# Token weights in two parts, q and k copied at once, and most turns of u and late x moved to DMA transposes, in a new order

## Chip, cores and metric

The kernel runs on one core of a Trainium2 chip. The metric is device time in microseconds of one execution. A profile shows one execution, which has its own time and a span from its first to its last instruction.

## What is computed

Chunked attention, then a mixing layer over tokens and channels. B = 8 batches, H = 8 heads, S = 576 tokens, D = 64; DM = H x D = 512.

```python
q_c, k_c, v_c = (t.reshape(B, H, 9, 64, D) for t in (q, k, v))       # 9 chunks of 64 tokens
attn = softmax(q_c @ k_c.transpose(0, 1, 2, 4, 3) / 8)
x = (attn @ v_c).reshape(B, H, S, D).transpose(0, 2, 1, 3).reshape(B, S, DM)
theta = x @ w_theta
y = einsum('ts,bsd->btd', w_tok_r, x * cos(theta)) + einsum('ts,bsd->btd', w_tok_i, x * sin(theta))
u = x + y
out = u + maximum(u @ w_ch, 0)
```

## The kernel before

The batches go in four pairs (p = 0 to 3). The 1152 tokens of a pair are 9 tiles of 128 rows, j = 0 to 8: tiles 0 to 3 are batch one, 5 to 8 batch two, tile 4 holds the last 64 tokens of each. Attention and theta work on groups of tiles: A is tiles 0 and 1, B 2 and 3, M the shared tile 4 alone, C 5 and 6, D 7 and 8. Everything that TensorE multiplies is fp16, sums are fp32 in PSUM.

The order of the work is written out by hand: `ORDER` is a list of steps `kind.pg.slot` (p the pair, g the group or tile, slot one of three wide PSUM buffers of two banks or of two thin ones of one bank). The program is built in this order, so each engine gets its instructions in it, and so does each DMA queue: POOL's (all loads that cast fp32 to fp16) and SP's (weights r, stores, moves, transposes). `tc.manual_schedule()` adds only the waits between engines. Buffers come from pools with fixed numbers of buffers; a tile waits until the one that held its buffer is done with.

The steps, with the lines of the profile:

- `q`, `k`, `v` (L174, L182): two POOL DMAs each, for one group. `lt`, `lc` (L202): the weights w_theta and w_ch.
- `lw.00` (L191, L192): w_tok_r comes as fp32 by SP's queue into wraw and wend; `cw` (L198, L199): ACT casts it into wnat. `lw.01` (L194, L195): w_tok_i comes as fp16 by POOL's queue.
- `init` makes the identity on POOL, `ones` fills constants on DVE, `new` takes x, zr, zi of a pair, `D` (L157) is two idle matmuls on a blank tile.
- `TW` (L225): 30 turns of token weights on TensorE into PSUM; `twd` (L241, L243) and `twa` (L241) copy them to wT by DVE and ACT.
- `T` (L259): turns q and k of a group on TensorE into one PSUM buffer, 32 small matmuls (16 for M). `tq` and `tk` (L277, L279) copy q by DVE and k by ACT (both by DVE for M) into two tiles.
- `S` (L290): scores, 32 small matmuls. `e` (L303): exponentials on ACT. `V0`, `V1` (L323): attention times v for four heads each, with a column of ones for the sums; `v0`, `v1` (L335, L336): reciprocal and product on DVE give x.
- `X` (L354), `x` (L366): turn of x on TensorE, 16 matmuls, and copy by ACT. `Xd` (L375): the same by one DMA transpose on SP's queue.
- `H` (L388): theta, 8 matmuls of 512 columns. `g` (L404, L408): cosine and sine on ACT. `z` (L417 to L426): zr and zi on DVE. `zm` (L431, L432): two SP DMAs bring half of the M tile to the other partitions.
- `Y` (L457): token product of one tile, 9 matmuls of 512 columns; for pair 0 in parts `Ya`, `Yb`, `Yc`. `y` (L465): u = x + y on DVE.
- `U` (L474), `u` (L491, L489): turn of u on TensorE, four matmuls, and copy by ACT (even tiles) or DVE (odd). `Ud` (L482): by one DMA transpose on SP's queue.
- `W` (L497): channel product, 4 matmuls. `w` (L506): relu and sum on DVE. `st` (L521): two SP stores of 128 KB each.

A Y needs zr and zi of all groups of its batch and of M, and all nine blocks of wT in its columns. Before, 16 of the 36 u and 15 of the 20 x groups are turned on TensorE, all q and k too.

Of the kernel before, what the change touches and what calls it, by code (L numbers as in the profile page):

```python
# [602 lines left out]
```

The softmax here doesn't subtract the row's maximum and nothing guards it: scores larger than these inputs give would overflow.

## Time and profile before

| | us |
|---|---|
| median of 3 runs (lowest, highest) | 212.73 (212.34, 214.2) |
| profiled execution: its time | 213.03 |
| profiled execution: span of its instructions | 210.7 |
| busy: TensorE, its weight loads | 191.4, 96.7 |
| busy: DVE, ACT, POOL | 123.6, 111.3, 104.4 |
| DMA: moved, at a mean of | 31.36 MB, 149 GB/s |

POOL's busy time is nearly all its work on 124 load DMAs. A matmul counts as busy from its issue to its modelled end, and they overlap, so the sum of the time of all matmuls is more than TensorE's pace. In the views, PE is TensorE, PEld its weight load, DVE the vector engine, ACT the scalar engine, POOL GpSimd, SP the engine that only issues DMAs; a "q" after a name is its sequencer. The row "PE" of the slices gives the busy share of TensorE in 40 equal slices of 5.27 us, in tenths; "PEclk" is the clock that it was granted, in tenths of full speed. The chain of waits is followed back from the last instruction, and is shown as start, length and what ran. The tile view gives for each engine and line the shortest, median and longest instruction in ns and the first and last start.

### The profile page before, as it was taken

How to read it: one execution, taken by the hardware profiler on the slowest of the kernel's cores; microseconds unless marked ns; L12 is line 12 of the kernel's file. 1: busy time of each engine (PE TensorE's matmuls, PEld its weight loads, DVE VectorE, ACT ScalarE, POOL GpSimd, SP SyncE). 2: the span in 40 equal slices, each digit the busy share in tenths (PEclk: the TensorE clock that was granted, in tenths of full speed). 3: DMA queues.
4: the chain of work that ended last, by engine and by line, in shares of the span. 5: the costliest groups of instructions: out<-in, count | busy, mean ns of one | idle time of the engine just before them, and what ended most of it. 6: DMA issues, size and time to landing. Idle time of an engine off the chain costs nothing.

```text
span 210.7 us, 6370 instructions
## 1 busy us (share of the span) xinstructions
PE 191.4 (91%) x2774; PEld 96.7 (46%) x2774; DVE 123.6 (59%) x240; ACT 111.3 (53%) x119; POOL 104.4 (50%) x130
## 2 busy tenths in 40 slices
PE   7678698897989999999999999999899988999981
PEld 2334444353545654555555545545544424444430
DVE  0014644663959675776884447849886365846451
ACT  2525469635886668777567668793260631500010
POOL 8997889988999898987997000000000000000000
PEclk9965579999999999999999999999999999999999
DMA  6999999999999999999999972423428687626875
GB/s 191 189 149 171 186 156 159 162 157 156 150 147 210 218 160 178 153 213 158 169 186 201 190 106 53 104 50 65 91 56 173 125 173 151 151 59 130 174 155 130
DMA packets 136858, 31.36 MB, mean 149 GB/s; under 512 B 129536, under 2 KB 131648, under 8 KB 136832
## 3 DMA queue, kind: packets, MB, share of 16 engines
q0 software_dynamic: 114176, 15.88, 119.6%
q1 hardware_dynamic: 22656, 15.10, 31.5%
q8 instruction: 21, 0.34, 0.7%
q14 instruction: 5, 0.04, 0.1%
HBM read 33.06 MB, written 9.44 MB: 202 GB/s over the span
## 4 chain that ended last, share of the span: by engine, by line
PE 65%; DVE 9%; ACT 9%; DMA 7%; POOL 6%; issue 1%; SPq 0%; POOLq 0%; ACTq 0%
PE ps_y L457 27%; PE ps_theta L388 14%; PE ps_uw L497 13%; POOL qk L174 5%; DMA v<-in_v_dram 4%; PE ps_x L323 3%; DMA xT<-x 3%; ACT kT L277 3%; PE ps_qkT L259 3%; PE ps_sT L290 2%; DVE qT L277 2%; PE ps_xT L354 2%; DVE x L336 2%; ACT xT L366 1%; PE ps_uT L474 1%
## 5 line engine op out<-in xcount | busy, mean ns | idle before, releaser
L457 PEld LDWEIGHTS <-wT 128*128 128x128 f16 (+1 forms) x360 | 30.7, 100 | 34.4 <-issue 0.8
L457 PE MATMUL ps_y<-zr,wT 128*128 128x512 f16 (+1 forms) x180 | 44.4, 381 | 0.0
L457 PE MATMUL ps_y<-zi,wT 128*128 128x512 f16 (+1 forms) x180 | 42.0, 379 | 0.0
L465 DVE TENSOR_TENSOR u<-ps_y,x 128x512 f16<-128x512 f32 x36 | 24.7, 690 | 27.9 <-PE ps_y L457 27.8
L497 PE MATMUL ps_uw<-wch,uT 128*128 128x512 f16 x144 | 36.3, 380 | 1.2 <-ACT uT L491 0.7
L388 PE MATMUL ps_theta<-wtheta,xT 128*128 128x512 f16 x144 | 36.0, 393 | 1.4 <-DMA xT<-x 1.0
L174 POOL DMA_DIRECT2D qk<-in_q_dram x40 | 34.2, 875 | 4.9 <-issue 1.4
L174 POOL DMA_DIRECT2D qk<-in_k_dram x40 | 34.1, 870 | 2.7 <-DMA wnat<-in_moe_w_tok_i_dram 0.8
L182 POOL DMA_DIRECT2D v<-in_v_dram x40 | 34.1, 879 | 2.3 <-DMA qk<-in_k_dram 0.6
L506 DVE SCALAR_TENSOR_TENSOR o<-ps_uw,u 128x512 f32<-128x512 f32 x36 | 24.8, 689 | 15.8 <-PE ps_uw L497 15.5
L404 ACT ACTIVATE cos<-ps_theta,pihalf 128x1024 f16<-128x1024 f32 (+1 forms) x20 | 20.6, 1032 | 21.4 <-PE ps_theta L388 14.9
L303 ACT ACTIVATE eT<-ps_sT 128x1024 f16<-128x1024 f32 (+1 forms) x20 | 18.5, 939 | 16.9 <-PE ps_sT L290 16.8
L336 DVE TENSOR_TENSOR x<-ps_x,recip 128x512 f16<-128x512 f32 (+1 forms) x40 | 25.5, 638 | 1.4
L388 PEld LDWEIGHTS <-xT 128*128 128x128 f16 x144 | 13.7, 100 | 17.9 <-issue 2.1
L497 PEld LDWEIGHTS <-uT 128*128 128x128 f16 x144 | 13.0, 98 | 16.6 <-DMA uT<-u 1.3
L366 ACT COPY xT<-ps_xT 128x1024 f16<-128x1024 f16 (+1 forms) x15 | 13.9, 931 | 12.2 <-PE ps_xT L354 12.1
L277 ACT COPY kT<-ps_qkT 128x1024 f16<-128x1024 f16 x16 | 16.1, 1018 | 7.7 <-DVE qT L277 4.4
L408 ACT ACTIVATE sin<-ps_theta 128x1024 f16<-128x1024 f32 (+1 forms) x20 | 18.7, 937 | 0.0
L491 ACT COPY uT<-ps_uT 128x512 f16<-128x512 f16 x9 | 5.3, 592 | 24.3 <-PE ps_uT L474 24.2
L277 DVE COPY qT<-ps_qkT 128x1024 f16<-128x1024 f16 x16 | 11.0, 688 | 9.3 <-ACT kT L277 6.6
L259 PE MATMUL ps_qkT<-id,qk 64*128 64x64 f16 x576 | 12.8, 196 | 2.1 <-DMA qk<-in_k_dram 1.3
L335 DVE RECIPROCAL recip<-ps_x 128x8 f32<-128x8 f32 (+1 forms) x40 | 7.9, 197 | 10.5 <-PE ps_x L323 10.2
(43 smaller groups left out, 153.5 us busy)
## 6 DMA issues: line engine op xcount, KB each, us to landing
out_dram<-o SPq DMA_DIRECT2D x72, 128.0 KB, 2.4
qk<-in_q_dram POOLq DMA_DIRECT2D x32, 128.0 KB, 6.2
qk<-in_k_dram POOLq DMA_DIRECT2D x32, 128.0 KB, 6.5
v<-in_v_dram POOLq DMA_DIRECT2D x32, 128.0 KB, 6.7
wraw<-in_moe_w_tok_r_dram SPq DMA_DIRECT2D x1, 1152.0 KB, 5.8
wnat<-in_moe_w_tok_i_dram POOLq DMA_DIRECT2D x1, 576.0 KB, 7.7
qk<-in_q_dram POOLq DMA_DIRECT2D x8, 64.0 KB, 6.4
qk<-in_k_dram POOLq DMA_DIRECT2D x8, 64.0 KB, 6.1
```

The source lines that it names most:

```text
L174: nc.gpsimd.dma_start(nats[p, g][rows, which, r], (q, k)[which][b, :, t0 : t0 + n, :].rearrange("h s d -> s h d"),)
L182: nc.gpsimd.dma_start(v16[rows, slot + r, :, 0:D], v[b, :, t0 : t0 + n, :].rearrange("h s d -> s h d"),)
L259: nc.tensor.transpose(psv[:, r, w, e, j, :], t[half[r], w, j, 2 * e : 2 * e + 2, :].rearrange("s h d -> s (h d)"), id16[half[r], half[r]],)
L277: copy(out=t.rearrange(flat), in_=ps.rearrange(flat))
L336: nc.vector.tensor_tensor(out=st[p]["x"][:, j0 : j0 + n, f * NE * D : (f + 1) * NE * D].rearrange("p c (h d) -> p c h d", h=NE), in0=psv[: ...
L388: nc.tensor.matmul(ps[:, j * DM : j * DM + DM], xT[:, j * NDB + db, :], wtheta16[:, db, :], start=(db == 0), stop=(db == NDB - 1),)
L404: nc.scalar.activation(out=cos[:, 0:n].rearrange("p a e -> p (a e)"), in_=pin, func=AF.Sin, bias=pihalf, scale=1.0,)
L408: nc.scalar.activation(out=sin[:, 0:n].rearrange("p a e -> p (a e)"), in_=pin, func=AF.Sin)
L457: nc.tensor.matmul(ps[rows], wT[:, kt, cols], z[:, jz, :], start=(kt == 0), stop=(kt == 2 * KT),)
L465: nc.vector.tensor_tensor(out=u, in0=st[p].pop(("ps_y", j))[:, 0:DM], in1=st[p]["x"][:, j], op=ALU.add)
L497: nc.tensor.matmul(ps, uT[:, db * P : db * P + P], wch16[:, db, :], start=(db == 0), stop=(db == NDB - 1),)
L506: nc.vector.scalar_tensor_tensor(out=o, in0=st[p].pop(("ps_uw", j)), scalar=0.0, in1=u, op0=ALU.max, op1=ALU.add)
```

## The change

- `load_tok` loads both token weights on POOL's queue, as fp16, in two parts: part 0 (`lw.00`, `lw.01`) holds output tokens 0 to 255, part 1 (`lw.02`, `lw.03`) tokens 256 to 575, with a second DMA for the last 64. The SP loads, wraw, wend and the cast on ACT go.
- `tok_w` turns one part in two steps (`TW.00` to `TW.03`: 16, 20, 24 and 30 matmuls); `tok_w_copy` copies them on DVE alone.
- `qk_copy` copies q and k by one instruction into one tile qkT, by DVE (`tq`, 8 groups) or ACT (`tqa`, 8). The q and k of 3A to 3D are transposed by one SP DMA each (`Td`) from the loaded tile.
- x: 8 of 20 groups are turned on TensorE, copied by ACT (`x`, 4) or DVE (`xv`, 4), and 12 are DMA transposes. u: tile 34 is turned on TensorE, the other 35 by DMA transposes.
- `D` is one idle matmul, and there are 60 (before 14 of two).
- Buffers: nat 8 (before 7), u16 7 (6), uT 5 (4), qkT 4 and 2 (before 3 and 2 each of qT and kT).
- The order is new. POOL loads q of A, B, C, M, k of A and B, w_theta and k of M before it makes the identity; the token weights follow after v.0B.

The first and last lines of the old order are shown, and the whole of the new one.

```diff
--- before.py
+++ after.py
@@ ORDER @@
-ones.00 D.00.0 lw.00 cw.00 D.00.1 init.00 D.00.0 D.00.1 q.0M q.0B q.0A D.00.0 k.0M
-D.00.1 D.00.0 D.00.1 k.0B TW.00.0 twa.00 k.0A D.00.0 T.0M.1 tk.0M D.00.1 D.00.0 tq.0M
-S.0M.2 e.0M lt.00 T.0B.1 T.0A.2 tk.0A tq.0B D.00.1 tq.0A tk.0B S.0A.2 v.0M V1.0M.1 v.0A
-e.0A D.00.0 V0.0M.2 twd.00 S.0B.0 new.00 v1.0M V1.0A.1 v0.0M V0.0A.2 v0.0A v.0B q.1M
-v1.0A lw.01 X.0M.2 e.0B V1.0B.0 X.0A.1 v1.0B x.0M H.0M.2 V0.0B.0 x.0A v0.0B q.0C k.1M
-v.0C H.0A.1 g.0M X.0B.0 z.0M zm.0M x.0B g.0A TW.02.2 H.0B.0 T.1M.1 twa.02 twd.02 TW.01.2
...
-y.36 w.35 W.32.0 w.32 st.35 Ud.36 Y.34.1 y.34 Y.33.0 W.37.1 y.33 W.36.0 w.37 Y.38.1
-st.32 Ud.34 w.36 Ud.33 y.38 st.37 W.34.0 w.34 W.33.1 w.33 st.36 st.34 st.33 U.38.0 u.38
-W.38.1 w.38 st.38 D.00.0
+ones.00 new.00 D.00.0 q.0A D.00.1 D.00.0 D.00.1 D.00.0 D.00.1 D.00.0 q.0B D.00.1 D.00.0
+q.0C D.00.1 D.00.0 D.00.1 D.00.0 D.00.1 q.0M D.00.0 k.0A D.00.1 D.00.0 D.00.1 k.0B
+D.00.0 D.00.1 D.00.0 D.00.1 D.00.0 D.00.1 lt.00 D.00.0 k.0M D.00.1 D.00.0 D.00.1 D.00.0
+D.00.1 D.00.0 D.00.1 D.00.0 D.00.1 D.00.0 init.00 T.0A.0 T.0B.1 tq.0A v.0A S.0A.2 D.00.1
+D.00.0 k.0C tqa.0B v.0M D.00.1 v.0B D.00.0 D.00.1 q.1M lw.02 q.0D D.00.0 D.00.1 S.0B.0
+T.0M.1 tq.0M D.00.0 e.0A V0.0A.2 S.0M.1 e.0B e.0M V1.0A.0 T.0C.1 v0.0A lw.03 v1.0A
+V0.0M.2 D.00.1 D.00.0 lw.01 v0.0M lw.00 V1.0M.0 v1.0M X.0A.2 k.0D xv.0A v.0C tqa.0C
+X.0M.0 V0.0B.1 q.1D V1.0B.2 new.10 v0.0B v.0D D.00.1 q.1C k.1M x.0M H.0M.0 H.0A.1 v1.0B
+X.0B.2 g.0M TW.02.0 k.1D x.0B D.00.0 z.0M g.0A twd.02 v.1M q.1A H.0B.2 k.1C D.00.1
+TW.03.0 z.0A D.00.0 lc.00 twd.03 g.0B z.0B Ya.02.1 S.0C.1 TW.01.2 q.2M TW.00.0 v.1D v.1C
+q.1B twd.00 twd.01 k.2M zm.0M Yb.02 k.1A Yc.02 Ya.01.0 Yb.01 y.02 T.0D.0 e.0C V0.0C.1
+v0.0C v.2M V1.0C.2 Yc.01 Ya.00.1 Yb.00 v1.0C tqa.0D k.1B v.1A X.0C.1 S.0D.2 xv.0C Yc.00
+Ud.02 y.01 e.0D V0.0D.0 v0.0D V1.0D.1 v1.0D H.0C.2 q.2A v.1B X.0D.0 T.1M.1 g.0C y.00
+D.00.0 D.00.1 xv.0D Ud.01 D.00.0 H.0D.0 tq.1M S.1M.1 Ya.03.1 D.00.0 z.0C g.0D Yb.03
+Yc.03 e.1M T.1D.2 tqa.1D z.0D v.2A T.1C.0 Y.06.0 tq.1C S.1C.1 V1.1M.0 y.03 y.06 v1.1M
+S.1D.2 Y.08.1 k.2A e.1C V0.1M.0 q.2B y.08 e.1D V1.1D.1 V0.1D.2 Y.07.0 q.2D Ud.00 v0.1D
+v1.1D q.2C v0.1M k.2B W.02.1 V0.1C.2 V1.1C.1 y.07 w.02 X.1M.0 v1.1C k.2D W.01.0 W.00.1
+Ud.06 Xd.1D x.1M H.1M.0 T.2M.1 Ud.07 v0.1C g.1M w.01 tq.2M T.1A.2 tq.1A Y.05.0 Ud.03
+S.2M.1 S.1A.2 q.3M st.02 w.00 Ud.08 k.2C T.1B.0 Y.04.1 e.2M Xd.1C y.05 tq.1B v.2B e.1A
+st.01 st.00 V1.1A.1 q.3C V0.1A.0 v.2D v0.1A S.1B.2 W.06.0 H.1D.0 e.1B v.2C g.1D y.04
+v1.1A X.1A.2 xv.1A V0.1B.1 W.03.1 k.3M H.1A.2 v0.1B w.06 H.1C.1 g.1A w.03 Ud.05 V1.1B.0
+z.1M W.07.0 v1.1B w.07 W.08.1 V0.2M.2 X.1B.0 w.08 g.1C z.1D st.06 z.1C st.03 T.2A.1
+zm.1M x.1B tqa.2A q.3B W.05.0 H.1B.0 w.05 v.3M g.1B Y.15.1 Ud.04 y.15 new.20 v0.2M z.1B
+st.07 Y.18.0 st.05 k.3C y.18 S.2A.1 T.2D.0 q.3D T.2B.2 Ud.15 st.08 Ud.18 W.04.1 tq.2B
+e.2A tqa.2D Y.17.0 V1.2A.1 z.1A S.2B.2 w.04 V1.2M.0 v1.2M Y.14.1 v1.2A T.2C.0 Xd.2M y.17
+e.2B y.14 Ud.14 st.04 V0.2A.2 v0.2A tqa.2C V0.2B.1 Y.11.0 q.3A S.2C.2 v0.2B S.2D.1 y.11
+V1.2B.0 W.18.1 w.18 W.15.0 Xd.2A Y.16.1 v1.2B k.3B T.3M.0 e.2D V0.2D.1 Ud.11 e.2C w.15
+V1.2D.2 Y.10.0 tqa.3M Ud.17 y.16 v1.2D y.10 st.15 st.18 k.3D H.2M.0 W.14.1 Y.13.0 w.14
+Xd.2B Ud.10 g.2M Ud.16 v0.2D Xd.2D Td.3C V1.2C.2 y.13 S.3M.1 k.3A V0.2C.0 v1.2C W.11.1
+Y.12.0 st.14 w.11 H.2A.2 W.17.1 st.11 Ud.13 v0.2C g.2A v.3D H.2B.0 Xd.2C y.12 Ud.12 v.3B
+z.2M W.16.0 w.17 g.2B w.16 st.17 W.13.1 z.2B H.2D.2 H.2C.0 z.2A zm.2M Td.3B new.30 w.13
+Y.22.0 g.2D y.22 Y.21.1 g.2C z.2C e.3M st.16 y.21 st.13 Td.3A W.10.0 V0.3M.2 v.3C w.10
+Td.3D S.3B.0 e.3B z.2D st.10 S.3C.1 e.3C Ud.21 Y.23.1 W.12.0 V1.3M.0 y.23 V0.3B.1 Ud.22
+Ud.23 v0.3M v0.3B v1.3M Y.20.1 w.12 S.3A.2 V0.3C.1 y.20 st.12 V1.3C.0 W.21.0 v0.3C w.21
+Y.25.1 st.21 v1.3C Ud.20 W.22.0 v.3A y.25 W.23.1 w.22 S.3D.1 e.3A V1.3B.2 Xd.3M V0.3A.0
+v0.3A v1.3B st.22 Y.24.0 w.23 Ud.25 st.23 y.24 e.3D V1.3D.1 V0.3D.0 V1.3A.2 v1.3A Y.26.1
+v0.3D y.26 Xd.3B Ud.26 v1.3D Xd.3C W.25.0 H.3M.2 w.25 Y.28.1 Xd.3A y.28 st.25 H.3B.0
+Ud.24 Xd.3D W.20.0 W.26.1 g.3M z.3M w.26 Ud.28 g.3B z.3B H.3A.1 w.20 st.20 Y.27.1 st.26
+g.3A y.27 Ud.27 H.3D.2 z.3A g.3D W.28.0 zm.3M w.28 z.3D W.24.1 H.3C.0 w.24 Y.33.0 st.24
+y.33 W.27.1 w.27 st.28 g.3C Ud.33 Y.30.0 y.30 Ud.30 z.3C st.27 Y.31.1 y.31 Ud.31 Y.32.0
+y.32 Ud.32 W.30.1 w.30 Y.38.0 y.38 W.33.1 st.30 w.33 st.33 W.32.0 Ud.38 w.32 Y.36.1 y.36
+Ud.36 W.31.0 w.31 st.31 st.32 Y.37.1 y.37 Y.35.0 W.36.1 y.35 w.36 Ud.37 Y.34.0 W.38.1
+y.34 Ud.35 W.35.0 w.38 w.35 W.37.1 U.34.0 uv.34 st.36 W.34.0 w.37 D.00.1 D.00.1 D.00.1
+st.38 w.34 D.00.0 st.35 D.00.1 st.37 D.00.0 D.00.1 st.34
@@ -112,7 +112,7 @@
     thin = ctx.enter_context(
         tc.tile_pool(name="thin", bufs=1, space=bass.MemoryType.PSUM)
     )
-    nat = ctx.enter_context(tc.tile_pool(name="nat", bufs=7))
+    nat = ctx.enter_context(tc.tile_pool(name="nat", bufs=8))
     tmp = ctx.enter_context(tc.tile_pool(name="tmp", bufs=3))
     pairp = ctx.enter_context(tc.tile_pool(name="pairp", bufs=1))
     outp = ctx.enter_context(tc.tile_pool(name="outp", bufs=4))
@@ -131,8 +131,6 @@
     wch16 = glob.tile([P, NDB, DM], FP16, name="wch16")
     wT = glob.tile([P, 2 * KT + 1, S], FP16, name="wT")
     wnat = glob.tile([P, KT + 1, 2, S], FP16, name="wnat")
-    wraw = pairp.tile([P, KT, S], FP32, name="wraw")
-    wend = glob.tile([CH, S], FP32, name="wend")
     blank = const.tile([P, DM], FP16, name="blank")
     v16 = glob.tile([P, 2 * NT, H, VP], FP16, name="v16")
 
@@ -153,8 +151,7 @@
 
     def idle(p, i, slot):
         ps = psum1("ps_idle", slot)
-        for r in range(2):
-            nc.tensor.matmul(ps, blank[:, 0:P], blank, start=True, stop=True)
+        nc.tensor.matmul(ps, blank[:, 0:P], blank, start=True, stop=True)
 
@@ -184,66 +181,61 @@
                 v[b, :, t0 : t0 + n, :].rearrange("h s d -> s h d"),
             )
 
-    def load_tok(ri):
+
+
+    def load_tok(i):
+        part, ri = divmod(i, 2)
         ap = (moe_w_tok_r, moe_w_tok_i)[ri]
-        aps = ap[0 : KT * P, :].rearrange("(a p) s -> p a s", p=P), ap[KT * P : S, :]
-        if ri == 0:
...
+        nc.gpsimd.dma_start(
+            wnat[:, 2 * part : 2 * part + 2, ri],
+            ap[part * GT : part * GT + GT, :].rearrange("(a p) s -> p a s", p=P),
+        )
+        if part:
+            nc.gpsimd.dma_start(wnat[0:CH, KT, ri], ap[KT * P : S, :])
 
     def load_w(ap, f16):
         nc.gpsimd.dma_start(f16, ap.rearrange("(a p) e -> p a e", p=P))
 
-    def tok_w(k3, slot):
+
+
+    def tok_w(i, slot):
+        part = i // 2
+        kts = range(KT) if i % 2 == 0 else range(KT, 2 * KT + 1)
+        n = len(kts)
         ps = psum2("ps_wT", slot, FP16)
-        for k in range(3):
-            kt = 3 * k3 + k
...
+        main = ps[:, 0 : n * GT].rearrange("p (k x) -> p k x", k=n)
+        middle = ps[:, 5 * GT : 5 * GT + n * CH].rearrange("p (k x) -> p k x", k=n)
+        for tbs in ((0, 1),) if part == 0 else ((2, 3), (KT,)):
+            for k, kt in enumerate(kts):
+                for tb in tbs:
+                    rows = slice(0, P if tb < KT else CH)
+                    if tb < KT:
+                        to = main[:, k].rearrange("p (c r x) -> p c r x", c=2, r=2)
+                        to = to[:, :, tb % 2]
                     else:
-                        ri, s0 = h, KT * P
-                    nc.tensor.transpose(
...
+                        to = middle[:, k]
+                    for h in range(2):
+                        if kt < 2 * KT:
+                            ri, jl = kt // KT, kt % KT
+                            s0 = (jl // 2) * GT + (jl % 2) * CH + h * P
+                        else:
+                            ri, s0 = h, KT * P
+                        nc.tensor.transpose(
+                            to[half[h]],
+                            wnat[rows, tb, ri, s0 : s0 + CH],
+                            id16[rows, rows],
+                        )
+        st["wT", i] = main, middle
+
+    def tok_w_copy(i):
+        main, middle = st["wT", i]
+        part = i // 2
+        ks = slice(0, KT) if i % 2 == 0 else slice(KT, 2 * KT + 1)
+        nc.vector.tensor_copy(out=wT[:, ks, part * GT : part * GT + GT], in_=main)
+        if part:
+            nc.vector.tensor_copy(out=wT[:, ks, KT * P : S], in_=middle)
 
@@ -265,22 +257,37 @@
                         )
         st[p]["ps_qkT", g] = psv
 
-    def qk_copy(p, g, which):
+    def qk_tile(n):
+        return tmp.tile(
+            [P, 4 * NE * n * CH], FP16, name="qkT", tag=f"qkT{n}",
+            bufs=4 if n == 2 else 2,
+        )
+
+
+
+    def qk_copy(p, g, copy):
         n = 1 if g == "M" else 2
-        ps = st[p]["ps_qkT", g][:, :, which]
-        name = "qk"[which] + "T"
-        t = tmp.tile([P, 2, NE, n, CH], FP16, name=name, tag=f"{name}{n}", bufs=n + 1)
-        st[p][name, g] = t
-        copy = nc.scalar.copy if which and n == 2 else nc.vector.tensor_copy
-        if n == 2:
-            flat = "p r e j c -> p r (e j c)"
-            copy(out=t.rearrange(flat), in_=ps.rearrange(flat))
+        ps, t = st[p]["ps_qkT", g], qk_tile(n)
+        tv = t.rearrange("p (r w e j c) -> p r w e j c", r=2, w=2, e=NE, j=n)
+        if n == 1:
+            flat = "p r w e c -> p (r w e) c"
+            copy(out=tv[:, :, :, :, 0].rearrange(flat), in_=ps[:, :, :, :, 0].rearrange(flat))
         else:
-            copy(out=t[:, :, :, 0], in_=ps[:, :, :, 0])
+            copy(out=t, in_=ps.rearrange("p r w e j c -> p (r w e j c)"))
+        st[p]["qkT", g] = lambda hs, w, e, j, r: tv[hs, r, w, e, j, :]
+
+    def qk_dma(p, g):
+        t = qk_tile(2)
+        nc.sync.dma_start_transpose(
+            t.rearrange("p (a c) -> p a c", c=P),
+            nats.pop((p, g)).rearrange("p w j h d -> p (w j h d)"),
+        )
+        tv = t.rearrange("p (w j e r c) -> p w j e r c", w=2, j=2, e=NE, r=2)
+        st[p]["qkT", g] = lambda hs, w, e, j, r: tv[hs, w, j, e, r, :]
 
     def scores(p, g, slot):
         n = 1 if g == "M" else 2
-        qT, kT = st[p].pop(("qT", g)), st[p].pop(("kT", g))
+        t = st[p].pop(("qkT", g))
         ps = psum2("ps_sT", slot)
         psv = ps.rearrange("p (h j e c) -> p h j e c", h=2, j=2, e=NE)
         for j in range(n):
@@ -289,8 +296,8 @@
                     for r in range(2):
                         nc.tensor.matmul(
                             psv[half[r], h, j, e, :],
-                            kT[half[h], r, e, j, :],
-                            qT[half[h], r, e, j, :],
+                            t(half[h], 1, e, j, r),
+                            t(half[h], 0, e, j, r),
                         )
         st[p]["ps_sT", g] = ps
 
@@ -358,12 +365,12 @@
                     )
         st[p]["ps_xT", g] = psv
 
-    def x_copy(p, g):
+    def x_copy(p, g, copy):
         n = 1 if g == "M" else 2
         psv = st[p].pop(("ps_xT", g))
         xT = tmp.tile([P, 2 * NDB, P], FP16, name="xT")
         st[p]["xT", g] = xT
-        nc.scalar.copy(
+        copy(
             out=xT[:, 0 : n * NDB].rearrange("p a (r c) -> p r a c", r=2), in_=psv
         )
 
@@ -460,7 +467,7 @@
                 )
 
     def add_x(p, j):
-        u = tmp.tile([P, DM], FP16, name="u16", bufs=6)
+        u = tmp.tile([P, DM], FP16, name="u16", bufs=7)
         st[p]["u", j] = u
         nc.vector.tensor_tensor(
             out=u, in0=st[p].pop(("ps_y", j))[:, 0:DM], in1=st[p]["x"][:, j], op=ALU.add
@@ -477,18 +484,15 @@
         st[p]["ps_uT", j] = psv
 
     def u_dma(p, j):
-        uT = tmp.tile([P, DM], FP16, name="uT", bufs=4)
+        uT = tmp.tile([P, DM], FP16, name="uT", bufs=5)
         st[p]["uT", j] = uT
         nc.sync.dma_start_transpose(uT.rearrange("p (a c) -> p a c", a=NDB), st[p]["u", j])
 
-    def u_copy(p, j):
-        uT = tmp.tile([P, DM], FP16, name="uT", bufs=4)
+    def u_copy(p, j, copy):
+        uT = tmp.tile([P, DM], FP16, name="uT", bufs=5)
         st[p]["uT", j] = uT
         psv = st[p].pop(("ps_uT", j))
-        if j % 2:
-            nc.vector.tensor_copy(out=uT, in_=psv)
-        else:
-            nc.scalar.copy(out=uT, in_=psv)
+        copy(out=uT, in_=psv)
 
     def w(p, j, slot):
         uT = st[p].pop(("uT", j))
@@ -529,16 +533,15 @@
         "lt": lambda p, g: load_w(moe_w_theta, wtheta16),
         "lc": lambda p, g: load_w(moe_w_ch, wch16),
         "lw": lambda p, i: load_tok(i),
-        "cw": lambda p, i: cast_tok(),
         "init": lambda p, g: setup(),
         "ones": lambda p, g: fill(),
         "new": lambda p, g: pair(p),
         "TW": lambda p, i, slot: tok_w(i, slot),
-        "twd": lambda p, i: tok_w_copy(i, 0),
-        "twa": lambda p, i: tok_w_copy(i, 1),
+        "twd": lambda p, i: tok_w_copy(i),
         "T": qk_t,
-        "tq": lambda p, g: qk_copy(p, g, 0),
-        "tk": lambda p, g: qk_copy(p, g, 1),
+        "Td": qk_dma,
+        "tq": lambda p, g: qk_copy(p, g, nc.vector.tensor_copy),
+        "tqa": lambda p, g: qk_copy(p, g, nc.scalar.copy),
         "S": scores,
         "e": exps,
         "V0": lambda p, g, slot: attn(p, g, 0, slot),
...
+        "ua": lambda p, j: u_copy(p, j, nc.scalar.copy),
+        "uv": lambda p, j: u_copy(p, j, nc.vector.tensor_copy),
```

## The prediction

> **What bounds the kernel now.** I read the page first: the busy shares, then the slices.
>
> ```profile
> PE 191.4 (91%) x2774; PEld 96.7 (46%) x2774; DVE 123.6 (59%) x240; ACT 111.3 (53%) x119; POOL 104.4 (50%) x130
> ...
> PE   7678698897989999999999999999899988999981
> ...
> PEclk9965579999999999999999999999999999999999
> DMA  6999999999999999999999972423428687626875
> ```
>
> TensorE is the bound from about 62 us on (9s); before that it is not full, its clock is low from slice 3 to 6, and the DMA engines are full until slice 23 (about 120 us), when the last load lands. Two stages, then: a start that waits for loads, and a long stretch in which TensorE's own work sets the pace.
>
> The chain of waits in order of time prices the steps, since back to back steps follow each other there without a gap:
>
> ```profile
> 102.39 0.86 PE ps_uw L497 x4
> 103.26 0.34 PE ps_xT L354 x16
> ...
> 104.94 0.22 PE ps_uT L474 x4
> ...
> 106.49 1.02 ACT kT L277
> ...
> 107.54 0.70 DVE qT L277
> 108.24 0.04 issue
> 108.28 1.89 PE ps_theta L388 x8
> ...
> 130.19 0.57 PE ps_qkT L259 x32
> ...
> 132.34 1.73 PE ps_theta L388 x8
> ...
> 190.53 1.94 PE ps_y L457 x9
> ```
>
> A token product Y (9 matmuls) is 1.94, a theta H (8) 1.73, a channel product W (4) 0.86 to 0.87, a turn of q and k T (32) 0.57, of x X (16) 0.34, of u U (4) 0.22 to 0.23; from other rows of this chain scores S (32) are 0.38 to 0.39, one attention half V (16) 0.25 to 0.26. Groups M cost about half. The three rows at 106.49 to 108.28 show a real stall: kT is copied by ACT, then qT by DVE, one after the other, and theta stands behind.
>
> I lay these prices along the order. From the first token product at 36.71 to the last W at 204.85 the steps add up to 157.6 us; the stretch took 168.1. So 10.5 us are lost there: 3.9 by T.1D at 61.6, 6.0 by 118, 1.2 more at 148 and 2.0 between 165 and 175. The span is 36.7 (start) + 157.6 + 10.5 + 5.9 (last W, add, store, end) = 210.7.
>
> Last, the DMA side: the tile view of uT and the page's issue list.
>
> ```profile
> L482 SPq DMA_TRANSPOSE uT<-u x20: 1188/1213/2321, 114.6 to 199.9; - x20
> ...
> DMA to landing us min/median/max: 2.4/2.4/6.6
> ```
>
> A transpose of u lands 2.4 us after its issue once the loads are over, but the first, issued at 114.6 among them, took 6.6. SP spends 1.2 us on each.
>
> **What the Trainium skill says.** "DMA: Bandwidth & Descriptors", section "Issuing engines are not separate DMA queues": DMAs from SP, ACT and POOL run on the same 16 engines and interleave. The trace agrees: out stores land mostly in 2.2 to 2.5 us after 124, in 5.1 to 7.6 during the loads. The same page, section "SWDGE vs HWDGE vs iDMA": a cast needs GpSimd's queue, a transpose SP's or ACT's; in the trace the fp16 loads are all POOL's, the transposes all SP's. "TensorE: Matmul & The Clock Gate", section "What's actually happening": the array's clock is halved until recent activity releases it. In the windows view the granted clock is 0.50 from 12.35 to 29.42, and the 12 theta matmuls from 25.5 on take 1.82 + 2.69 = 4.5 us in the chain instead of 0.86 + 1.73.
>
> **The change, part by part.**
>
> Turns removed from TensorE. U falls from 16 to 1: 15 x 0.23 = 3.45. X falls from 12 full and 3 M to 6 full and 2 M: 6 x 0.34 + 0.20 = 2.24. T falls from 16 full to 12: 4 x 0.57 = 2.28. Token-weight turns stay 90 transposes. Sum 8.0 us off the 172.2 us of all steps without idle ones. Those after 62 us lie on the full engine and count whole.
>
> Copies. ACT loses the 16 kT (16.1), most x copies (13.9 to about 3.2), 9 uT (5.3), wT (2.4) and the cast of the weights (2.8, and a table load). It gains 7 copies of 2048 columns; by the slope of its rows (597 ns at 512, 1018 at 1024) one is about 1.86, and one M copy of 1.02: 14.0. ACT 111 becomes about 88. DVE loses 19.7 and gains 4 x 1.23 (slope 417 to 688), 3 x 0.69, wT 3.6, x 2.8, u 0.4, so 13.8: 124 becomes 118. Neither bounds. The one-instruction copy takes 1.23 or 1.86 where the pair in turn took 1.72, so T to S is no longer; it only loses the wait between engines (6.6 + 4.4 us in the list of waits, partly under TensorE work). Larger tiles (nat 8, u 7, uT 5, four qkT) cost no time; wraw's room pays.
>
> DMA transposes: 35 u, 12 x and 4 qk of 2048 columns. SP: 35 x 1.2 + 12 x 1.3 + 4 of an unseen length, at least 1.3 and by columns 2.6 to 5, + 80 plain issues x 0.6 = about 115 to 125 of 200 us, so SP isn't full; behind a late one stand stores and transposes. In the built order every SP DMA also waits for the landing of the one eight before it, at 6.6 us latency 8 in 6.6 us, above the need. Between u's add and its W, or x's norm and its H, the new order leaves 6 to 16 us during the loads and 3.5 to 14 after; an Ud needs 6.6 + 1.2 and then 2.4 + 1.2. I find few that are short by 1 to 2 us (W.13, H.2C, H.3B, H.3A, W.35). This I leave in the losses below.
>
> Their share of the loads' engines is not shown by the trace. From below: hidden in the gaps, 0. From above: a u transpose has 512 packets and a full load 1024, spaced 0.88 us, so 0.44 each, or 0.88 if a packet of 256 bytes counts twice. Up to 92 us the order issues 12 u and 2.5 x, so 7.5 us (15 at the dear end). POOL, too, waits for the landing of its load eight before: landings past 7 us slow the loads. Taking the old landings by position for the new list, the loads lie 0 to 3 us ahead of use up to T.2D without any loss, and 5 to 9 with the start and losses that I take. So I count 1 us for 0.44.
>
> Token weights. r no longer comes by SP at 0.7 to 7.3 us beside the first loads, with 2.8 us of ACT work; r and i come by 6 POOL DMAs (before 2), about 0.8 each, behind 25 loads: 4 x 0.8 = 3.2 us more in POOL's queue, with every later load behind them. Token turns move from 8.7 to behind 33 us; half of them (1.8 us) now falls after the first Y.
>
> The start, in POOL's order. The identity is made after 15 loads, near 13.6; T.0A follows near 14.2, S.0A near 16.6, v.0A lands near 22 (as before, 20.9 to 22.4), v.0M near 26, v.0B near 28.5. V0.0B and V1.0B stand ahead of H.0M, so thetas begin near 30 instead of 25.5. ACT then has table 1.3, g.0M 1.3, x.0B 1.0, g.0A 2.1; token turns TW.02 and TW.03 need weights that land near 32 and 35.5. The first Y comes at 38 with a fast clock, 40.3 if thetas run at half clock again (34 idle matmuls keep it up only until about 11). I take 39: 2.3 later than before, with fewer token turns and one more T done.
>
> The sum. From Ya.02 to W.34 the steps add up to 152.1 (157.6 less U 3.45, X 2.24, T 2.50, plus turns 1.8 and four idle matmuls 0.86). Losses: before 10.5, of which some 2 are small change between steps. Fewer ACT to DVE hand-overs and no wait for uT copies should take off 2.5; loads behind transposes add 1: 9. Tail 5.9 as before, since U.34 and its copy stand there like U.38. Span 39 + 152.1 + 9 + 5.9 = 206.0. The profiled execution was 213.03 for a span of 210.7, so + 2.3: 208.3; it lay 0.3 above the median of the runs, so 208.0.
>
> **Rivals.**
> A (forecast, 0.48): as summed, losses 7 to 11: 206 to 210.
> B (0.20): hand-overs go almost entirely, clock warm at the start: 38 + 152.1 + 5.5 + 5.9 = 201.5, time 203.5. For it: ACT falls by 23 us and the chain holds ACT and DVE for 18%. Against: the load slack is thin until 92 us.
> C (0.17): the late thetas run cold, weights land late, first Y at 41.5 and losses 11: 210.5, time 212.5, unchanged. The change then moves work from the stretch to the start.
> D (0.15), slower: the transposes take the loads' place on the DMA engines. Place: from Ud.02 (about 47) to the last load. At 0.88 per u, the loads of T.2D are 15 us late against 9 of slack, 6 lost, and the 6 further u, 4 x and one qk before the loads end add 1 to 2: span 213, time 215. It decides from about 0.7 us per u transpose. For it: the first u transpose took 6.6, and landings rise from 5.8 to 7.7 when 10 SP DMAs come within 9 us (60 to 69). Against: these ten, of 64 to 128 KB as one u is 128, cost 1.9 of later landing and 1.2 of POOL waits, 0.3 each.
>
> **How the numbers follow.** The time is A's, 208.0. A's own range is 206 to 210. To hold 8 in 10 I go from B's centre, 203, to 214.5, short of D's centre: a half of B's and somewhat more than a half of D's chance lie outside. About 1% is what a measurement can tell from no change: below 210.6 is faster, A and B but for a margin: 0.67; above 214.9 slower, D: 0.16; the rest 0.17.
>
> **What would show it.** In the changed profile the first ps_y matmul at 38 to 40; u transposes landing in 5 to 8 us before 120 and 2.4 after; the page's ACT near 88, DVE near 118; PE at 9s from about slice 9 with few waits for ps_x or qkT; the last load landing at 124 to 130. D would show as PE waits for DMA qk or v between 60 and 100 and a last landing past 140; C as a low clock over the thetas and a first Y after 41. I am wrong if the stretch from first Y to last W isn't near 161.

## The result, and the profile after

The changed kernel takes 240.28 us (median of 4, 239.62 to 242.75), the kernel before beside it 212.53 (4 runs): ratio 1.132, 95% interval 1.121 to 1.143. It is 13% slower; 2% faster was forecast. The profiled execution took 239.62, its span is 237.8. Ratios here leave disturbed executions out, so for e12 below ratio and median stand apart, e8 has no ratio, and the profiles of these two are of disturbed executions (e12's of 215.65).

The page: busy shares, then the slices (5.95 us each).

```profile
PE 195.2 (82%) x2514; PEld 92.7 (39%) x2514; DVE 120.1 (50%) x222; ACT 87.4 (37%) x84; POOL 106.9 (45%) x134
...
PE   7847899994999869906999964069979899999994
...
PEclk9988799997699999975899995558999999999999
DMA  7999999999999999999999999999986787555666
```

ACT fell as meant, and TensorE has 260 instructions less. But its 9s have holes up to slice 27 (160 us), at the deepest ones the clock falls to 5, and the DMA engines are at 9 to slice 29 (about 172 us; before, to slice 23, about 121). The last packet of a load comes at 165.6; before, at 121.4.

The shares of the chain of waits by engine, before and after, and rows of the chain after:

```profile
PE 65%; DVE 9%; ACT 9%; DMA 7%; POOL 6%; issue 1%; SPq 0%; POOLq 0%; ACTq 0%
```

```profile
DMA 41%; PE 39%; POOL 12%; issue 2%; DVE 2%; ACT 1%; SPq 1%; ACTq 0%; POOLq 0%
...
79.97 15.88 DMA qk<-in_q_dram
96.15 13.11 DMA qk<-in_k_dram
...
124.49 8.64 DMA uT<-u
...
134.41 9.80 DMA uT<-u
...
144.26 1.90 PE ps_uw L501 x4
...
149.81 6.85 DMA uT<-u
...
156.71 1.89 PE ps_uw L501 x4
158.59 5.45 PE ps_theta L395 x16
```

DMA had 7% of the chain, and has 41%. First loads hold it, 29 us in a row, then u transposes, 6.85 to 9.80 each. Two of the W that follow take 1.9 instead of 0.86, and 16 theta matmuls 5.45 instead of 3.46: the granted clock was 0.50 in the last wait (146.1 to 156.7 us) and 0.60 in the 7 us after it. So this wait of 10.6 us costs 3.0 more in the W and the thetas behind it.

The list of what TensorE waited for (us in total, times, longest), the tile view of uT, and the page's issue list, before and after (last column: median us from issue to landing):

```profile
PE ps_uw L501 <- DMA uT<-u: 13.8, 4, 10.6
PE ps_qkT L251 <- DMA qk<-in_k_dram: 12.7, 6, 6.6
```

```profile
L489 SPq DMA_TRANSPOSE uT<-u x35: 1188/1278/2973, 40.6 to 226.1; - x35
...
DMA to landing us min/median/max: 2.4/6.2/9.8
```

```profile
qk<-in_k_dram POOLq DMA_DIRECT2D x32, 128.0 KB, 6.5
v<-in_v_dram POOLq DMA_DIRECT2D x32, 128.0 KB, 6.7
```

```profile
qk<-in_k_dram POOLq DMA_DIRECT2D x32, 128.0 KB, 8.6
v<-in_v_dram POOLq DMA_DIRECT2D x32, 128.0 KB, 8.9
```

Both sides are late: the loads of k and v take 8.6 and 8.9 (before 6.5 and 6.7). The 18 transposes of u that are issued before the last load packet take 6.2 to 9.8, the 17 after it 2.4 to 4.3; before the change 17 of the 20 came after the loads.

Along the order, with the prices of the prediction, the first Y starts at 36.1 and the last W at 231.4; between them lie 152.1 of steps and 43.2 of losses, which is time beyond the steps' prices. The losses stand at 9.1 at 86 us; 9.2 come at once at T.2B (110 us, loads of 2B), 11.6 at W.13 (157 us, transpose of u.13).

### The profile page after: what moved, and what is told of

The parts are those of the page before. It is cut to its first block, busy times and chain, and to the rows that moved or that the text cites. A ratio compares the mean times of both kernels' runs of the same rounds, so it can differ in the third digit from the quotient of the medians.

```text
span 237.8 us, 5842 instructions
## 1 busy us (share of the span) xinstructions
PE 195.2 (82%) x2514; PEld 92.7 (39%) x2514; DVE 120.1 (50%) x222; ACT 87.4 (37%) x84; POOL 106.9 (45%) x134
## 4 chain that ended last, share of the span: by engine, by line
DMA 41%; PE 39%; POOL 12%; issue 2%; DVE 2%; ACT 1%; SPq 1%; ACTq 0%; POOLq 0%
PE ps_y L464 18%; DMA uT<-u 14%; DMA qk<-in_k_dram 13%; PE ps_uw L501 11%; POOL qk L171 9%; DMA qk<-in_q_dram 7%; PE ps_theta L395 6%; DMA xT<-x 4%; DMA wtheta<-in_moe_w_theta_dram 3%; POOL v L179 1%; PE ps_sT L297 1%; PE ps_qkT L251 1%; POOL wnat L189 1%; ACT eT L310 1%; PE ps_x L330 1%
## 5 line engine op out<-in xcount | busy, mean ns | idle before, releaser
L501 PE MATMUL ps_uw<-wch,uT 128*128 128x512 f16 x144 | 38.4, 400 | 14.4 <-DMA uT<-u 13.8
L464 PE MATMUL ps_y<-zr,wT 128*128 128x512 f16 (+1 forms) x180 | 46.4, 392 | 0.1
L464 PEld LDWEIGHTS <-wT 128*128 128x128 f16 (+1 forms) x360 | 31.7, 102 | 37.6 <-issue 5.3
L464 PE MATMUL ps_y<-zi,wT 128*128 128x512 f16 (+1 forms) x180 | 43.4, 388 | 0.0
L395 PE MATMUL ps_theta<-wtheta,xT 128*128 128x512 f16 x144 | 37.2, 406 | 2.3 <-DMA xT<-x 2.3
L251 PE MATMUL ps_qkT<-id,qk 64*128 64x64 f16 x448 | 11.1, 199 | 16.6 <-DMA qk<-in_k_dram 12.7
L276 ACT COPY qkT<-ps_qkT 128x2048 f16<-128x2048 f16 x7 | 13.1, 1865 | 28.0 <-PE ps_qkT L251 28.0
L276 DVE COPY qkT<-ps_qkT 128x2048 f16<-128x2048 f16 x5 | 6.1, 1222 | 27.5 <-PE ps_qkT L251 27.5
L154 PE MATMUL ps_idle<-blank 128*128 128x512 f16 x60 | 18.4, 443 | 1.3 <-DVE pihalf L142 1.2
L251 PEld LDWEIGHTS <-qk 64*128 64x128 f16 x448 | 8.8, 100 | 20.3 <-DMA qk<-in_k_dram 13.6
L342 DVE RECIPROCAL recip<-ps_x 128x8 f32<-128x8 f32 (+1 forms) x40 | 7.9, 196 | 11.7 <-PE ps_x L330 11.4
```

The lines of the kernel that those rows point to most:

```text
L251: nc.tensor.transpose(psv[:, r, w, e, j, :], t[half[r], w, j, 2 * e : 2 * e + 2, :].rearrange("s h d -> s (h d)"), id16[half[r], half[r]],)
L276: copy(out=t, in_=ps.rearrange("p r w e j c -> p (r w e j c)"))
L395: nc.tensor.matmul(ps[:, j * DM : j * DM + DM], xT[:, j * NDB + db, :], wtheta16[:, db, :], start=(db == 0), stop=(db == NDB - 1),)
L464: nc.tensor.matmul(ps[rows], wT[:, kt, cols], z[:, jz, :], start=(kt == 0), stop=(kt == 2 * KT),)
L501: nc.tensor.matmul(ps, uT[:, db * P : db * P + P], wch16[:, db, :], start=(db == 0), stop=(db == NDB - 1),)
```

## The experiments

Theory 1: loads and transposes together are more than the DMA engines carry in time, so each makes the other late. Theory 2: the transposes are late by themselves, by SP's order and their own length. Theory 3: the new order, weights or copies lose the time.

**Undoing a part of the transposes.** Turns on TensorE and their copies go back into the new order, well ahead of their use.

```diff
 e1: 18 u of pairs 0 and 1      e2: x of 1D, 1C, 2A to 2D, 2M   e3: q, k of 3A to 3D
-Ud.13                          -Xd.2B                          -Td.3C
+U.13.0 uv.13                   +X.2B.0 xv.2B                   +T.3C.2 tq.3C
 e4: e1, e2 and e3 together
```

> The changed kernel, but the 18 u of pairs 0 and 1 are turned on TensorE and copied, instead of by DMA transposes. T1 (each DMA transpose takes about 1 us of the loads' time on the DMA engines, so q, k and v land late and TensorE starves): 18 x 1.1 = 20 us less, last load lands near 145 instead of 165, time 222 to 228. T2 (the transposes only land late themselves, behind the loads and in SP's order, and W waits for them): the W waits of 14 us go, the last load stays past 158, time 224 to 228. T3 (order, weights or copies lose the time): 236 to 242, plus 4 us of turns.

> The changed kernel, but the x of 1D, 1C and pair 2 are turned on TensorE and copied; u and late q, k stay DMA transposes. T1: 6.5 transposes of double size, 13 x 1.1 = 14 us less for the loads, last load near 150, time 226 to 232. T2: only the 2 us of theta waits for x go, last load past 158, time 236 to 239. T3: 240 to 243.

> The changed kernel, but q and k of 3A to 3D are turned on TensorE and copied. T1: two of these four came before the last load, 8 u sizes, so last load near 156, time 233 to 237. T2 (SP held 2.7 to 5.6 us by each of these, 17 us in all, with transposes of u and x behind): W waits after 137 fall by 8 to 10 us, time 228 to 232. T3: no change, 239 to 242.

> The three together: no DMA transpose before pair 2's u; later u and pair 3's x stay DMA transposes. T1 and T2: last load at 120 to 126, few waits for loads or uT, time 205 to 212. T3: 225 or more.

| | time | ratio (interval) | last load packet |
|---|---|---|---|
| after | 240.28 | 1.132 (1.121, 1.143) | 165.6 |
| e1 | 229.89 | 1.081 (1.075, 1.086) | 137.7 |
| e2 | 230.10 | 1.083 (1.075, 1.090) | 156.2 |
| e3 | 238.91 | 1.122 (1.116, 1.129) | 160.9 |
| e4 | 247.51 | 1.154 (1.146, 1.162) | 125.3 |

e1 and e2 gain 10 us each, e3 about 1, which is within its interval: u and x count, q and k hardly. Only two of the four transposes of q and k are issued before the last load packet, at 141.5 and 158.0. In e1 the last load comes 28 us earlier, which theory 2 had excluded, though the time lies above the range of either. e4 frees the loads (125.3), and is the slowest: theories 1 and 2 had said 205 to 212, and it lies where theory 3 had put it, at 225 or more. Its slices and its longest waits:

```profile
PE   8757999999779688996696785953699999999984
...
DMA  8999999999999999999972210600325587745766
```

```profile
ACT uT L497 <- PE ps_uT L483: 33.3, 8, 10.2
...
ACT qkT L278 <- PE ps_qkT L253: 21.2, 5, 13.8
```

The DMA engines have little to do from slice 22 to 30, and TensorE is full of small gaps. They come evenly (4.5 us of losses by 72, 20 by 138, 40 at the end), and ACT and DVE wait long for turns that TensorE has not reached. I read this as an order laid out for transposes that loses by itself when turns are put back by hand; no run with an order of its own for them shows it. So e4 shows that with the new order, the token weights and the copies, but without the transposes, the loads end only 4 us later than before; it says nothing on what early loads are worth.

**Adding transposes to the kernel before.** Idle ones into a spare tile that nobody reads, one (e5) or two (e6) per u; e7 copies the same u in 512 pieces of 256 bytes, without turning.

```diff
+        e = st["extra"][0][:, st["extra"][1] % 8]
+        nc.sync.dma_start_transpose(e.rearrange("p (a c) -> p a c", a=NDB), st[p]["u", j])
 e7:
+        nc.sync.dma_start(e[:, :, 0:P], st[p]["u", j].rearrange("p (a c) -> p a c", a=NDB))
```

> The kernel before, plus 11 DMA transposes of u (128x512, fp16) into a spare tile that nobody reads, each issued when its u is ready, between 45 and 110 us. Nothing waits for them but the reuse of u. T1 (about 1.1 us of the loads' time each): last load at 131 to 134 instead of 120.5; the old order has 9 to 25 us of slack, so time 212.5 to 215. T2 (loads unharmed): last load at 120 to 123, time 212 to 213.5.

> As the dose of 11, with each u transposed twice: 22. T1: last load at 142 to 148, slack used up by k.2A, k.2B and v.2A, time 216 to 226. T2: last load at 120 to 125, time 212 to 215.

> As the dose of 22, but each is a plain SBUF to SBUF copy of the same u in 512 pieces of 256 bytes. If it is the packets, whatever they do: as the 22 transposes. If it is the transpose: last load at 120 to 131, time 212 to 215.

| | time | ratio (interval) | last load packet |
|---|---|---|---|
| e5, 11 | 215.33 | 1.013 (1.011, 1.016) | 142.1 |
| e6, 22 | 227.67 | 1.068 (1.059, 1.076) | 154.2 |
| e7, 22 plain | 217.23 | 1.022 (1.014, 1.029) | 145.1 |

This is theory 1 in the kernel before: transposes that nobody waits for make its loads 21 and 33 us late, and the end with them once the slack is used up.

The price is an estimate. Counted in windows of 2.5 us, the load queue finishes 1167 packets per us where SP is silent, and each 256-byte packet of SP's takes the place of 1.9 of them in the changed kernel, 2.3 in e5, 2.2 in e6, and 1.7 in e7. A u has 512, so a transpose takes 0.83 to 1.0 us of the loads' time. Other ways of counting spread further. A straight line through such windows gives 1.3 to 1.8 packets, about 0.6 to 0.8 us. The end of the loads gives more, and it came later than theory 1 had said, too: before the last load packet lie 14.0 u sizes in e5 and 25.0 in e6, against 1.4 in the kernel before, so the 20.7 and 32.8 us are 1.6 and 1.4 for each added one. About 1 us is all that can be said.

Plain pieces (e7) delay the loads by 24 us where transposes delay them by 33, and cost 2.2% where those cost 6.8%. So the turning isn't needed for the harm, but adds to it. Whether the rest is the small pieces or only the bytes isn't shown: no run copied u in large pieces.

**Fewer packets per load.** q and k read in rows of 2 KB.

```diff
-                (q, k)[which][b, :, t0 : t0 + n, :].rearrange("h s d -> s h d"),
+                (q, k)[which][b].rearrange("h s d -> (h s d)")[t0 * DM : (t0 + n) * DM]
+                .rearrange("(s h d) -> s h d", h=H, d=D),
```

> The changed kernel with one difference: q and k are read in rows of 2 KB that lie together (the first elements of the same batch, in memory order) instead of 64-element rows of eight heads, so a full load of q or k has 128 packets instead of 1024; v is loaded as before. The attention is then of other values than the reference's. Order, turns, copies and all DMA transposes are untouched. Theory 1 (the transposes' small packets take the loads' time on the DMA engines, and the late loads cause the losses): with q and k packets gone the loads end near POOL's own pace, about 110 to 125, the transposes land earlier, and most of the 34 us of unforeseen losses go: 206 to 216, and not slower than the same edit of the kernel before by more than 2%. Theory 2 (SP's order and the transposes' own time are what comes late) and theory 3 (the order, weights and copies lose the time whatever the loads do): 228 or more, and at least 8% above the same edit of the kernel before.

> The kernel before with the same edit: q and k read in rows of 2 KB that lie together, so that the attention is of other values than the reference's. It is the base for the kernel above. Its loads end at POOL's pace, about 105 to 120. All theories: its stretch had only some 4 us of waits for loads, so 207 to 212.

e8 lay between 226.08 and 237.84 (median of 4: 232.99), too spread for a ratio, and its last load came at 150.1 instead of 165.6. Theory 1's numbers failed (206 to 216, loads until 110 to 125); the time lies where theories 2 and 3 had put it. e9: 212.27, 0.998 (0.995, 1.001), last load at 117.5 instead of 121.4.

DMA slices of e9 (5.27 us each), and POOL's row for v from its page (after the last bar: its idle time, and who ended most of it):

```profile
DMA  6999999999999999279999742423428687626875
...
L183 POOL DMA_DIRECT2D v<-in_v_dram x40 | 34.4, 884 | 12.5 <-PE ps_x L324 11.4
```

But for two slices they stand at 9 as before. The windows view shows more: its last two numbers are the mean busy share of the DMA engines, which passes 1 where packets overlap, and GB/s. First before, then e9:

```profile
10.00:50.00 40.00, 33.23 (x645) 18.23 (x643) 20.12 (x46) 22.03 (x25) 34.82 (x43) 0.79 2.42 162
```

```profile
10.00:50.00 40.00, 30.59 (x617) 16.63 (x616) 19.80 (x46) 22.03 (x25) 30.99 (x49) 0.87 1.48 177
```

The share fell from 2.42 to 1.48 while the rate rose from 162 to 177 GB/s, and k lands in 5.1 us instead of 6.5. So the edit did make the loads lighter. That they end little sooner is no sign against it: they run so far ahead that POOL waits 11.4 us in one piece, until 92, for a buffer of v that TensorE still reads, and this is what the two slices show. In e8 TensorE's waits for q and k nearly go (12.7 us for k in the changed kernel), but those for v grow from 3.0 to 8.0, and those for transposes stay (uT 13.7 for 13.8, xT 4.6 for 2.3). Why lighter loads of q and k help the transposes so little is open. The two runs don't support theory 1 in the form that they tested, in which the number of packets is what a load costs.

**Fewer loads.** The same transposes and SP order, 37 of 120 load sizes left out.

```diff
+        if which and (p, g) in SAME:      # pairs 1 and 2, and 3M
+            return
 ...
+        if p >= 2:                        # load_v
+            return
 ...
-                            t[half[r], w, j, 2 * e : 2 * e + 2, :].rearrange(
+                            t[half[r], 0 if same else w, j, 2 * e : 2 * e + 2, :].rearrange(
```

> The changed kernel with 37 of its 120 load sizes left out: k of pairs 1 and 2 and of 3M is not loaded (q is turned twice in its place), v of pairs 2 and 3 is not loaded (that of pairs 0 and 1 stays), so the attention of those is of other values than the reference's. All DMA transposes, their order and all steps of TensorE stay. 37 x 0.88 is 33 us of the loads' time. Theory 1 (loads and transposes together are more than the DMA engines can carry in time): most of the 34 us of losses go, 206 to 218. Theory 2 (SP's order and the transposes' own time): u.13 still stands behind the long transpose of 3C, 226 or more.

> The kernel before with the same loads left out (k of pairs 1, 2 and 3M, v of pairs 2 and 3), so its attention is of other values too. Base for the kernel above. Its waits for loads in the stretch were some 4 us: 206 to 212.

e12: median 215.32, ratio 1.002 (0.999, 1.006); e13: 212.49, 0.999 (0.996, 1.001). By the ratios, about 33 us of loads taken away (37 at 0.88, an estimate) gave some 27 us back to the changed kernel and none to the kernel before. Theory 1 had said 206 to 218, theory 2 226 or more. The slices, the uT view and two of TensorE's waits in e12:

```profile
PE   7959699999977888999999986996699999999993
...
DMA  7999999999999999999998887998555876555665
```

```profile
L495 SPq DMA_TRANSPOSE uT<-u x35: 1188/1240/2505, 42.0 to 202.2; - x35
...
DMA to landing us min/median/max: 2.4/2.5/9.6
```

```profile
PE ps_uw L507 <- DMA uT<-u: 6.5, 2, 3.7
...
PE ps_qkT L257 <- DMA qk<-in_k_dram: 0.3, 1, 0.3
```

All 35 transposes are there. Beside the loads, which now end at 106.6, they still take 5.6 to 9.6 to land, and after them 2.4 to 4.9; the median is 2.5 because most come after. This is the run that decides for theory 1, and against theory 3 for most of the loss, since order, weights and copies are all in it. Losses are 17 still, 11 of them at 130 to 157: u.13, and later u.21 and u.22, stand on SP right behind transposes of q and k. So a smaller part is SP's own, as theory 2 has it, and shows once the loads no longer cover it.

**SP's order alone.** The 2048-column transpose of 3C is needed only at 169 us, and u.13 stands behind it.

```diff
-... Ud.16 v0.2D Xd.2D Td.3C ... st.11 Ud.13 v0.2C ... Xd.2C y.12 Ud.12
+... Ud.16 v0.2D Xd.2D ... st.11 Ud.13 v0.2C ... Xd.2C y.12 Ud.12 Td.3C
```

> The changed kernel with one step moved: the transpose of q and k of 3C is issued after that of u.12 instead of ahead of st.14, st.11, u.13, x of 2C and u.12. It is needed only at 169 us. Theory 1: u.13 lands 6 to 9 us sooner, but the queue stays full and what stands behind is late in its turn: 232 to 238. Theory 2: the 11.6 us that W.13 lost are gained whole: 227 to 230.

242.03, ratio 1.135 (1.128, 1.142): no gain, and above the numbers of both theories. TensorE's waits from 40 to 170 us:

```profile
PE ps_qkT L250 <- DMA qk<-in_k_dram: 11.5, 7, 3.7
PE ps_uw L500 <- DMA uT<-u: 4.9, 1, 4.9
PE ps_y L463 <- DMA zr<-zmid: 3.8, 1, 3.8
```

W.13 loses 5 instead of 11.6, but others are late in its turn, and the losses add up to 44.3 (43.2 before the move). I read this as a queue whose sum is too large, which its order doesn't mend. Theory 2 falls as the main cause here, and so does my reading of W.13 as a fault of one place.

**Late transposes in the kernel before.** q and k of 3C, 3B and 3D, u.12, u.16 and x of 2B go to SP from about 115 us on (e17: only u and x). qkT lies in the room of wraw.

```diff
-T.3C.2 tk.3C tq.3C  T.3B.0 tq.3B tk.3B  T.3D.2 tq.3D tk.3D  U.12.1 u.12  U.16.0 u.16  X.2B.1 x.2B
+Td.3C               Td.3B               Td.3D               Ud.12        Ud.16        Xd.2B
 e16, order on SP: Ud.17 Ud.12 Ud.14 Ud.18 st.04 zm.2M Ud.16 st.17 Td.3C Xd.2B st.12 st.14 st.16 Td.3B Td.3D
```

> The kernel before with DMA transposes only where few loads are left: q and k of 3C, 3B and 3D, u.12 and u.16 and x of 2B turned by SP instead of TensorE, issued from about 118 us on; 2.5 us of TensorE steps less and three pairs of q and k copies less. Theory 1 (a transpose is harmless once the loads are through): 208.5 to 211, ratio 0.98 to 0.993. Theories 2 and 3: SP's 2.7 to 5.6 us for one of q and k delay u transposes and stores behind it, so 212 to 216.

> The kernel before with q and k of 3C, 3B and 3D, u.12 and u.16 and x of 2B turned by DMA from about 115 us on, as in e10, but each transpose is issued only when its tile is free, and u.14 and u.18 ahead of the stores: 2.5 us of TensorE steps less. Theory 1: once the loads are through (about 122) a transpose costs TensorE nothing: 208.5 to 211. Theory 2: a 2048-column transpose holds what stands behind it on SP, 213 to 217.

> The kernel before with q and k of 3C, 3B and 3D, u.12 and u.16 and x of 2B turned by DMA from about 115 us on, as in e15, but with the stores of tokens 17, 12, 14 and 16 issued ahead of the transposes of 3C, 3B and 3D. 2.5 us of TensorE steps less than before. Theory 1 (free once the loads are through, if nothing that is needed sooner stands behind them on SP): the 5 us at 135 to 140 go, 209 to 212, ratio 0.983 to 0.998. Theory 2 (the transposes' own length on SP is what costs): 215 or more.

> The kernel before with only u.12, u.16 and x of 2B turned by DMA, issued from about 115 us on; q and k all on TensorE. 0.8 us of TensorE steps less. Theory 1: 211 to 212.5, ratio 0.992 to 1.0. Theory 2: 213 or more.

e10: 222.98, 1.049 (1.044, 1.054). My order let the transpose of 3D write the tile of 3C before S.3C had read it, so S.3C used q and k of 3D and waited 6.5 us for them; this run says nothing on the question. e15: 217.03, 1.020 (1.013, 1.027), where theory 2 had put it (213 to 217). In it DVE waits once for a store, and the chain shows where:

```profile
DVE o L522 <- DMA out_dram<-o: 4.0, 1, 4.0
```

```profile
132.36 2.00 SPq L286
134.41 1.01 SPq L537
135.46 3.28 DMA out_dram<-o
...
138.86 0.69 DVE o L522
139.55 0.61 DVE zr L433
140.20 5.30 PE ps_y L473 x16
```

A store (L537) stands on SP behind the transpose of q and k (L286); DVE has no free output tile, zr stands behind that on DVE, and a Y behind zr. TensorE waits 3.1 us for this zr, and by the prices 4.7 are lost there. With the stores ahead, e16: 213.59, 1.003 (1.000, 1.005); e17: 212.72, 1.000 (0.997, 1.003). The stall went, as theory 1 said, but the forecast gain of 0.2 to 1.7% did not come: in e16's profile the steps sum to 155.1 instead of 157.6, and the losses rose from 10.5 to 12.0. Late transposes with nothing urgent behind them do no harm, and bring nothing that can be measured.

**The one-instruction copy alone**, in the old order, all on DVE:

```diff
-tk.0A tq.0B D.00.1 tq.0A tk.0B
+tq.0A tq.0B D.00.1
```

> The kernel before with q and k of a group copied by one instruction, all on VectorE (2048 columns at about 1.23 us for a full group) instead of kT on ScalarE and then qT on VectorE; nothing else. The part of the change that the copies are, alone: ScalarE loses 16.1 us, VectorE gains some 8. Theories 1 and 2: the turn from T to S no longer passes two engines, 0.5 us sooner a group: 210 to 213. Theory 3 (the copies slow the stretch): 215 or more.

212.21, 0.997 (0.995, 1.000): harmless, perhaps 0.3% faster. So the copy isn't the cause, and this part of theory 3 falls. No version measurably better than the kernel before, by 1%, was found.

## Why the prediction was wrong

The failed step is "So I count 1 us for 0.44" in the paragraph on the loads' engines. Instead of this 1 us, the losses came out 34.2 us above the 9 of the forecast, and e12 gives some 27 back where loads and transposes leave each other room. Three things were wrong in it.

The price. A u takes about 1 us of the loads (0.83 to 1.0 by the windows, 0.6 to 1.6 over all ways of counting), where 0.44 was taken and 0.88 was the upper bound. I had taken 256-byte packets as equal to a load's packets, or twice them. The argument for the low price (ten SP DMAs cost only 1.9 us of later landing) took a delay of landing for a share of the engines, and those ten were stores and moves, none a transpose.

The count. The list "12 u and 2.5 x up to 92 us" is 17 u sizes. At 0.96 (see below) they are 16 us, against the 5 to 9 of lead that I found: 7 to 11 lost; the trace has 9.1 at 86 us. But I stopped there. The "6 further u, 4 x and one qk" that rival D put at "1 to 2" are 18 more sizes, 17 us, and late loads draw further transposes into their phase: 37.8 u sizes lie before the last load packet (1.4 before the change). The loads end 44.2 us later; POOL's waits for buffers that TensorE holds explain 9.3 of it, and the other 34.9 over 36.4 added sizes are 0.96 each. This puts all the rest down to the transposes; it is no second measurement.

The other direction. Transposes beside loads were forecast at 5 to 8 us to landing, until about 120. They took 6.2 to 9.5 until 117, not far off; but late loads made that phase 45 us longer, and this return was not counted. Between 117 and 153 SP issues almost without a pause, its transposes take 6.8 to 11.4 us to land, and W.13, H.2B and W.16 wait. W.13 stood on the prediction's list of those short by 1 to 2 us, and lost 11.6. The Trainium skill, "DMA: Bandwidth & Descriptors", section "Queues, rings and completion order", says that each DMA engine takes turns between the queues that have work, packet by packet (a packet there is a group of descriptors, not one of the pieces counted here). The trace agrees in that both queues slow down while both are full (k 6.5 to 8.6, u 2.4 to 6.2 in the median), and each is quick without the other: k takes 6.3 in e4, u 2.4 to 4.3 after the last load.

Point by point:

- Steps 152.1: all matmuls of the new order are in the trace, and the stretch was priced with the same prices; the new copies are 1222 ns on DVE and 1865 on ACT for 1.23 and 1.86. ACT 87.4 for 88. DVE 120.1 for 118: it makes five full copies, not four, so the sum should have been 119.
- Start 39: it was 36.1, so 2.9 better; rivals B and C were both out on it. No run took the start apart.
- Tail 5.9: 6.4.
- Losses 9: 43.2. That is the whole error: with -2.9, +34.2 and +0.5 the span goes from 206.0 to 237.8.
- "SP isn't full": true of the whole span, but from 117 to 165 it issued for 44 of the 48 us. An average hid the stage.
- Last load at 124 to 130: 165.6. The forecast's own test failed: first Y to last W is 195.4, not 161.
- Rival D had the mechanism. Of its signs, the last landing past 140 came; between 60 and 100 there is one wait for a load, 2.0 us for v, and those for k lie at 54 to 58 and 101 to 109. Its 215 was short, since it priced one stretch and left the later sizes at nearly nothing, and the range ended just below it.

What stays open: how much of the 6 us of losses that e12 has beyond the kernel before is the new order, and how much that execution's own; why e8 gained so little; and what a good order without transposes would give, since e4's wasn't one.

## What to carry to other kernels

Before a turn is moved to a DMA, add up the DMA engines' demand over the stretch where it will run: loads, transposes and stores, each at its price, and with what late loads draw in; a 9 in the slices doesn't say what is left, as e9 has nearly the same 9s with loads that run far ahead. TensorE's 0.23 us for a u was cheaper than about 1 us of all 16 DMA engines while loads need them. What stands behind a long transpose on its queue counts too, stores above all, as they hold the output tiles.

## What the runs showed of the hardware

- A 256-byte piece from SBUF to SBUF took an estimated 1.9 to 2.3 times a load packet's place when turned (after, e5, e6), and 1.7 when not (e7).
- An eighth of the packets for q and k let k land in 5.1 us instead of 6.5, and the engines move 177 GB/s instead of 162 from 10 to 50 us (e9); the slices show 9 there in both.
- Beside loads a transpose of u landed 6.2 to 9.8 us after its issue, after the last load 2.4 to 4.3 (after).
- A transpose of 2048 columns kept SP for 1.5 to 3.2 us once the loads were over (e10, e15, e16), and for 5.6 beside them (after, at 141 us).
- A wait of TensorE is paid for again in part: after 10.6 us of idling, W took 1.89 for 0.86 and 16 theta matmuls 5.45 for 3.46, at a granted clock of 0.60 (after, at 157 to 164 us).
